# A linear-attention block on one core: reordered head loads, q tiles and normaliser spread over the state stage, a permuted Wo round trip, and a split last tile

## The chip, the cores and the metric

The kernel runs on one core of a Trainium2 chip. The metric is device time in microseconds (us). A profiled run also gives the span, from the first to the last instruction, which is 1.8 to 2.1 us shorter than the measured time; places in time below are us from the start of the span. TensorE does the matrix products, ScalarE the exponentials and part of the copies out of the accumulators, VectorE the rest; the sync engine (SP) and ScalarE issue transfers.

Each run of a changed kernel has runs of the kernel before beside it on the same chip. A run more than 1.5% above the fastest of its kernel is set aside as slow. Some kernels below do or do not fall to half TensorE clock in mid-kernel from run to run; for those I give the median of all runs as well, because the label then separates two behaviours of the kernel itself.

## The reference

```python
# x: (1, 2048, 640) bf16; wqkv: (640, 1920); wo: (640, 640); 32 heads of 20
qkv = (x @ wqkv) -> q, k, v per head
phi = lambda t: where(t > 0, t + 1, exp(t)) + 1e-6
kv  = einsum("bhsd,bhse->bhde", phi(k), v)
z   = sum over s of phi(k)
o   = einsum("bhqd,bhde->bhqe", phi(q), kv) / (einsum("bhqd,bhd->bhq", phi(q), z) + 1e-6)
out = o (heads joined) @ wo
```

## The kernel before

It never forms v. It sums P = x^T phi(k) over the rows (the state stage), gets kv = P^T Wv per group of six heads, masks it to 20x20 blocks, and folds it into Wo, so that the output is one product of the normalised phi(q) with the folded matrix. The stages on TensorE are: head (transposes of the first four row tiles, first key products), K stage (key products), state in two halves, kv and Wo groups with q tiles between them, output.

```python
def load_wk():                      # head loads on two queues
    for eng, what in (("act", "x0 w0 w2 w4 x2"), ("sp", "x1 w1 w3 x3")):
        ...                         # then the activation table

def p_step(h, st):                  # one state step: 5 products into banks 0 to 4
    for d in range(5): matmul(bank(d), xn[st, d], pk[st, half h])

def w2_rows():                      # folded Wo: to memory and back with rows regrouped
    dma(w2d[0:600] <- w2g[0:120, 5 groups]); dma(w2d[600:640] <- w2g[0:40, group 5])
    for c in range(5):
        dma(w2p[:, c] <- w2d.rearrange("(h c j) n -> c h j n", c=5, j=4)[c])

warm(5); transpose_x(0, 6); transpose_x(1, 7); warm(2)
for c in range(5):                  # first 20 key products, weight chunk by weight chunk
    for st in range(2):
        for h in range(2): k_half(st, h, (c,))
    if c >= 3: transpose_x(c - 1, c + 3)
```

The round trip through memory is there because the q side keeps its columns in the order (chunk c, head h, j) while the folded matrix comes out in the order (h, c, j).

Of the kernel before, what the change touches and what calls it, by code (L numbers as in the profile page):

```python
# [82 lines left out]
def bass_standalone__linear_attn_block__prompt_kernel(nc, x, wqkv, wo, out):  # L83
# [9 lines left out]
    BK = 512  # L93

    with contextlib.ExitStack() as ctx:
# [26 lines left out]
        bm = sb("bm", GW)  # L122
        ones = sb("ones", 8, F32)
# [23 lines left out]
        def pool_const():  # L147
# [10 lines left out]
            P.add("pool", lambda e: e.memset(bm[:, :], 1.0), writes=["bm"])  # L158
# [17 lines left out]
            for lo in (True, False):  # L176
                band(bm[:, :], [[-DH if lo else DH, NG], [0, DH]],
                     0 if lo else DH - 1, 1 if lo else -1, "bm")
# [8 lines left out]
        def load_xT():  # L187
            for i, (a, b) in enumerate(XCH[NPE:]):
                P.add("sp", lambda e, a=a, b=b: e.dma_start_transpose(
                    xT[:, :].rearrange("p (c s) -> p c s", s=S)[:, :, a:b], x[0, a:b, :]),  # L190
                    reads=[("wk", 0)] if i == 0 else [],
                    writes=[("xT", NPE + i)], dma=True)

        def transpose_x(st, b):
            v = bank(b, HALF).bitcast(BF16)

            def mm(e):
                for c in range(NC_):
                    r = e.transpose(v[:, 128 * c:128 * c + 128],  # L199
                                    xn[:, st * D + 128 * c:st * D + 128 * c + 128], ident[:, :])  # L200
                return r
            P.add("pe", mm, reads=[("xn", st), "ident"], writes=[("bank", b)])
            P.add("dve", lambda e: e.tensor_copy(  # L203
                xT[:, :].rearrange("p (c s) -> p c s", s=S)[:, :, 128 * st:128 * st + 128],
                v.rearrange("p (c s) -> p c s", s=128)),
                reads=[("bank", b)], writes=[("xT", st)])

        def xT_keys(a, b):
            return [("xT", i) for i, (p, q) in enumerate(XCH) if p < b and a < q]
# [13 lines left out]
        def load_wk():  # L223
            for eng, what in (("act", "x0 w0 w2 w4 x2"), ("sp", "x1 w1 w3 x3")):
# [8 lines left out]
            tl = mybir.InstLoadActFuncSet(  # L233
                name=nc.get_next_instruction_name(),
                act_func_set_id=ACT_TABLE_SET_LN_EXP, ins=[], outs=[])
            P.add("act", lambda e: e.add_instruction(tl), writes=["table"])
# [28 lines left out]
        def k_half(st, h, cs=range(NC_)):  # L265
# [10 lines left out]
            P.add("pe", mm, reads=xT_keys(128 * st, 128 * st + 128) + [("wk", c) for c in cs],  # L276
# [16 lines left out]
        def p_step(h, st):  # L293

            def mm(e):
                for d in range(NC_):
# [6 lines left out]
                  writes=[("bank", d) for d in range(NC_)])  # L303

        def p_out(h):
            for d in range(NC_):
                dst = pt[:, d * D + HALF * h:d * D + HALF * (h + 1)]
                if d % 2 == 0:
                    P.add("act", lambda e, d=d, dst=dst: e.copy(dst, bank(d, HALF)),  # L309
                          reads=[("bank", d)], writes=[("pt", d, h)])  # L310
                else:
                    P.add("dve", lambda e, d=d, dst=dst: e.tensor_copy(dst, bank(d, HALF)),
                          reads=[("bank", d)], writes=[("pt", d, h)])
# [70 lines left out]
        def kv_group(b):  # L384

            for lo, hi, bb in ((0, 4, b), (4, 6, b + 1)):
                def mm(e, lo=lo, hi=hi, bb=bb):
                    for g in range(lo, hi):
                        n = gsz[g]
                        m = 128 if g < 5 else n  # L390
                        for d in range(NC_):
# [3 lines left out]
                                pt[:, d * D + GW * g:d * D + GW * g + n],  # L395
# [5 lines left out]
            for lo, n, bb, w, key in ((0, 4, b, GW, 0), (4, 1, b + 1, GW, 1), (5, 1, b + 1, 40, 2)):  # L401
                src = ps[0:w, BK * bb + 128 * (lo % 4):BK * bb + 128 * (lo % 4) + 128 * n] \
                    .rearrange("p (g j) -> p g j", j=128)[:, :, 0:w]
                mk = bm[0:w, 0:w].unsqueeze(1).broadcast_to([w, n, w])
                dst = kvt[0:w, GW * lo:GW * (lo + n)].rearrange(
                    "p (g j) -> p g j", j=GW)[:, :, 0:w]
                P.add("dve", lambda e, src=src, mk=mk, dst=dst: e.tensor_tensor(
                    dst, src, mk, ALU.mult), reads=[("bank", bb), "bm"], writes=[("kvt", key)])

        def w2_group(g, b):  # L410
            n = gsz[g]
            for h in range(2):
# [3 lines left out]
                    reads=[("kvt", 0 if g < 4 else g - 3), "wog", "wog5"],  # L416
                    writes=[("bank", b + h)])
            P.add("act", lambda e: e.copy(
                fold(w2g[0:n, g * D:(g + 1) * D]), two_banks(b, parts=n)),
                reads=[("bank", b), ("bank", b + 1)], writes=[("w2g", g)])  # L420

        def w2_rows():
            P.add("sp", lambda e: e.dma_start(
                w2d[0:5 * GW, :].rearrange("(g p) n -> p g n", p=GW),
                w2g[0:GW, 0:5 * D].rearrange("p (g n) -> p g n", n=D)),
                reads=[("w2g", g) for g in range(5)], writes=["w2d"], dma=True)
            P.add("sp", lambda e: e.dma_start(
                w2d[5 * GW:D, :], w2g[0:gsz[5], 5 * D:6 * D]),
                reads=[("w2g", 5)], writes=["w2d5"], dma=True)
            for c in range(NC_):  # L430
                P.add("sp", lambda e, c=c: e.dma_start(
                    w2p[:, c * D:(c + 1) * D],
                    w2d.rearrange("(h c j) n -> c h j n", c=NC_, j=4)[c]),
                    reads=["w2d", "w2d5"], writes=[("w2p", c)], dma=True)
# [34 lines left out]
        def normalize(sbk):  # L469
            i = sbk % 2  # L470
            for c in range(NC_):
                v = pq[:, c * S + BK * sbk:c * S + BK * (sbk + 1)]
                P.add("dve", lambda e, v=v: e.tensor_tensor(v, v, rd[i][:, :], ALU.mult),  # L473
                      reads=[("rd", i), ("pq", sbk, c)], writes=[("pq", sbk, c)])

        def out_tile(st):
            b = 2 * (st % 4)
            j = st % 4
            for h in range(2):
                def mm(e, h=h):  # L480
                    for c in range(NC_):
                        r = e.matmul(bank(b + h, HALF),  # L482
                                     pq[:, c * S + 128 * st:c * S + 128 * st + 128],
                                     w2p[:, c * D + HALF * h:c * D + HALF * (h + 1)],
                                     start=(c == 0), stop=(c == NC_ - 1))
                    return r
                P.add("pe", mm, reads=[("pq", st // 4, c) for c in range(NC_)]
                      + [("w2p", c) for c in range(NC_)], writes=[("bank", b + h)])
            P.add("act", lambda e: e.copy(osb[j][:, 0:HALF], bank(b, HALF)),  # L489
                  reads=[("bank", b)], writes=[("osb", j, 0)])  # L490
            P.add("dve", lambda e: e.tensor_copy(osb[j][:, HALF:D], bank(b + 1, HALF)),  # L491
                  reads=[("bank", b + 1)], writes=[("osb", j, 1)])
            P.add("sp", lambda e: e.dma_start(
                out[0, 128 * st:128 * st + 128, :], osb[j][:, :]),
                reads=[("osb", j, 0), ("osb", j, 1)], writes=[("out", st)], dma=True)
# [7 lines left out]
        warm(5)  # L503
        transpose_x(0, 6)
        transpose_x(1, 7)
        warm(2)
        for c in range(NC_):
            for st in range(2):
                for h in range(2):
                    k_half(st, h, (c,))  # L510
            if c >= 3:
                transpose_x(c - 1, c + 3)
# [8 lines left out]
        qi = [0]  # L521

        def next_q(b):
            q_tile(*qs[qi[0]], b)
            qi[0] += 1

        for h in range(2):
            for st in range(NT):
                p_step(h, st)
                if zst and st % 2 == 1:  # L530
                    zst.pop(0)()
                if st == 7:
                    next_q(5 + qi[0] % 3)
            p_out(h)
            next_q(5 + qi[0] % 3)
            next_q(5 + qi[0] % 3)
        for f in zst:
            f()
        kv_group(0)
        next_q(5)  # L540
        z_finish(4)
        w2_group(0, 2)
        next_q(6)
        w2_group(1, 0)
        den(0, 4)
        den_act(0, 4)
        next_q(7)
        w2_group(2, 2)
        den_spread(0, 4)
        next_q(5)  # L550
        w2_group(3, 0)
        normalize(0)
        next_q(6)
        w2_group(4, 2)
        next_q(7)
        w2_group(5, 0)
        den(1, 4)
        w2_rows()
        den_act(1, 4)
        next_q(5)  # L560
        next_q(6)
        den_spread(1, 4)
        normalize(1)
        while qi[0] < 15:
            next_q((7, 2, 3, 5, 6)[qi[0] % 5])
        next_q(0)
        next_q(1)
        den(2, 4)
        den_act(2, 4)
        next_q(2)  # L570
        next_q(3)
        den_spread(2, 4)
        normalize(2)
        next_q(5)
        for st in range(2):
            out_tile(st)
        den(3, 6)
        den_act(3, 6)
        out_tile(2)
        den_spread(3, 6)  # L580
        normalize(3)
        for st in range(3, NT):
            out_tile(st)
# [4 lines left out]
        def _(e):  # L588
            P.emit("sp", e)
            for s in range(NT):  # L590
                op = P.writers[("out", s)]
# [45 lines left out]
```

## Time and profile before

| | before |
|---|---|
| time, median of 4 runs | 109.47 us |
| span of the profiled run | 107.7 us |
| TensorE busy, mean clock | 92%, 1.0 |
| first product of key tile 2 / first state product / first kv product | 9.19 / 29.03 / 57.56 |
| last q product done / first output product / last output product done | 81.00 / 81.00 / 104.86 |

The last two rows are milestones that I take from the timeline of TensorE. They are how the two kernels are compared below, because the work between two milestones can be counted. Their lines (start, length, group; the one at 9.19 is cut off by the end of its window):

```profile
5.88 2.38 PE L270 MATMUL ps<-wk,xT 128*128 128x320 bf16 x16
...
9.19 7.09 PE L270 MATMUL ps<-wk,xT 128*128 128x320 bf16 x51
...
29.03 5.61 PE L297 MATMUL ps<-pk,xn 128*128 128x320 bf16 x40 [0.66 <-DVE pk L288]
...
57.56 1.70 PE L392 MATMUL ps<-pt,wv 128*128 128x120 bf16 x30
...
79.92 1.24 PE L323 MATMUL ps<-xT,wqp 128*128 128x512 bf16 x5
81.00 2.88 PE L482 MATMUL ps<-w2p,pq 128*128 128x320 bf16 x20
```

### The profile page before, as it was taken

How to read it: one execution, taken by the hardware profiler on the slowest of the kernel's cores; microseconds unless marked ns; L12 is line 12 of the kernel's file. 1: busy time of each engine (PE TensorE's matmuls, PEld its weight loads, DVE VectorE, ACT ScalarE, POOL GpSimd, SP SyncE). 2: the span in 40 equal slices, each digit the busy share in tenths (PEclk: the TensorE clock that was granted, in tenths of full speed). 3: DMA queues.
4: the chain of work that ended last, by engine and by line, in shares of the span. 5: the costliest groups of instructions: out<-in, count | busy, mean ns of one | idle time of the engine just before them, and what ended most of it. 6: DMA issues, size and time to landing. Idle time of an engine off the chain costs nothing.

```text
span 107.7 us, 1890 instructions
## 1 busy us (share of the span) xinstructions
PE 99.6 (92%) x749; PEld 64.8 (60%) x755; DVE 68.2 (63%) x136; ACT 41.3 (38%) x77; POOL 10.7 (10%) x27
## 2 busy tenths in 40 slices
PE   5899999999799999999999999985999879999990
PEld 2467777777476674676767745432446557777760
DVE  1216998888899899701236674999879583333331
ACT  0404555555500206202035289872665433333330
POOL 6881000191000000000000000000000000000000
PEclk9999999999999999999999999999999999999999
DMA  2998999999980000000000000082730222333333
GB/s 52 370 203 190 223 145 213 383 366 363 266 161 0 0 3 0 0 0 6 0 0 3 0 0 6 14 215 75 194 111 0 85 104 85 119 117 125 118 120 115
DMA packets 16330, 12.24 MB, mean 114 GB/s; under 512 B 8386, under 2 KB 16322, under 8 KB 16322
## 3 DMA queue, kind: packets, MB, share of 16 engines
q1 hardware_dynamic: 15602, 11.31, 38.6%
q10 hardware_dynamic: 720, 0.82, 2.2%
q8 instruction: 6, 0.10, 0.4%
q14 instruction: 2, 0.02, 0.1%
HBM read 6.72 MB, written 3.44 MB: 94 GB/s over the span
## 4 chain that ended last, share of the span: by engine, by line
PE 75%; DVE 13%; ACT 5%; DMA 3%; issue 1%
PE ps L270 19%; PE ps L482 18%; PE ps L297 15%; PE ps L323 15%; DVE za L342 4%; DVE pq L336 3%; DMA xn<-in_x_dram 3%; ACT eq L331 3%; PE ps L199 2%; DVE pq L473 2%; PE ps L441 2%; PE ps L392 1%; DVE eq L333 1%; ACT rd L466 1%; PE ps L373 1%
## 5 line engine op out<-in xcount | busy, mean ns | idle before, releaser
L323 PE MATMUL ps<-xT,wqp 128*128 128x512 bf16 x94 | 22.9, 379 | 1.8 <-DVE pq L336 1.5
L297 PE MATMUL ps<-pk,xn 128*128 128x320 bf16 x160 | 22.4, 299 | 0.8 <-DVE pk L288 0.7
L482 PE MATMUL ps<-w2p,pq 128*128 128x320 bf16 x160 | 22.2, 299 | 0.7 <-ACT rd L466 0.7
L270 PE MATMUL ps<-wk,xT 128*128 128x320 bf16 x160 | 22.3, 299 | 0.0
L297 PEld LDWEIGHTS ps<-pk,xn 128*128 128x128 bf16 x160 | 15.5, 98 | 7.9 <-DVE pk L288 1.0
L331 ACT ACTIVATE eq<-ps 128x512 bf16<-128x512 f32 x20 | 11.9, 597 | 21.4 <-PE ps L323 21.3
L482 PEld LDWEIGHTS ps<-w2p,pq 128*128 128x128 bf16 x160 | 15.5, 98 | 7.0 <-ACT rd L466 0.8
L270 PEld LDWEIGHTS ps<-wk,xT 128*128 128x128 bf16 x160 | 15.7, 98 | 6.4 <-issue 0.6
L283 ACT ACTIVATE ek<-ps 128x640 bf16<-128x640 f32 x16 | 11.2, 704 | 13.5 <-PE ps L270 13.5
L323 PEld LDWEIGHTS ps<-xT,wqp 128*128 128x128 bf16 x100 | 9.3, 98 | 11.0 <-DVE pq L336 1.9
L491 DVE CAST osb<-ps 128x320 bf16<-128x320 f32 x16 | 7.8, 490 | 11.5 <-PE ps L482 11.5
L336 DVE SCALAR_TENSOR_TENSOR pq<-ps,eq 128x512 bf16<-128x512 f32 x20 | 13.8, 692 | 0.7
L288 DVE SCALAR_TENSOR_TENSOR pk<-ps,ek 128x640 bf16<-128x640 f32 x16 | 13.2, 825 | 0.5
L333 DVE TENSOR_SCALAR eq<-eq 128x512 bf16<-128x512 bf16 x20 | 5.8, 292 | 10.9 <-ACT eq L331 10.4
L489 ACT CAST osb<-ps 128x320 bf16<-128x320 f32 x16 | 6.8, 426 | 13.2 <-PE ps L482 13.1
L473 DVE TENSOR_TENSOR pq<-pq,rd 128x512 bf16<-128x512 bf16 x20 | 7.0, 418 | 0.3 <-ACT rd L466 0.3
L285 DVE TENSOR_SCALAR ek<-ek 128x640 bf16<-128x640 bf16 x16 | 5.4, 335 | 1.7 <-ACT ek L283 1.6
L203 DVE COPY xT<-ps 128x640 bf16<-128x640 bf16 x4 | 2.0, 492 | 6.7 <-PE ps L199 6.6
L309 ACT CAST pt<-ps 128x320 bf16<-128x320 f32 x6 | 2.2, 434 | 9.7 <-PE ps L297 9.7
L342 DVE TENSOR_TENSOR za<-pk 128x1280 f32<-128x1280 bf16 x4 | 5.7, 1484 | 0.0
L253 POOL COPY wqp<-wqn 128x640 bf16<-128x640 bf16 x5 | 3.7, 773 | 12.6 <-DMA wqn<-in_wqkv_dram 12.6
L261 PE MATMUL ps<-zero 128*128 128x512 bf16 x7 | 3.4, 630 | 1.3 <-DVE eps L155 1.3
(40 smaller groups left out, 47.6 us busy)
## 6 DMA issues: line engine op xcount, KB each, us to landing
out_dram<-osb SPq DMA_DIRECT2D x16, 160.0 KB, 1.8
xn<-in_x_dram SPq DMA_DIRECT2D x3, 640.0 KB, 7.7
wqn<-in_wqkv_dram SPq DMA_DIRECT2D x1, 800.0 KB, 5.3
wv<-in_wqkv_dram SPq DMA_DIRECT2D x1, 800.0 KB, 10.7
w2p<-w_rows SPq DMA_DIRECT2D x5, 160.0 KB, 2.7
wog<-in_wo_dram SPq DMA_DIRECT2D x1, 750.0 KB, 13.0
w_rows<-w2g SPq DMA_DIRECT2D x1, 750.0 KB, 5.3
wk<-in_wqkv_dram ACTq DMA_DIRECT2D x3, 160.0 KB, 3.9
```

The source lines that it names most:

```text
L270: r = e.matmul(bank(b + h, HALF), xT[:, c * S + 128 * st:c * S + 128 * st + 128], wk[:, c * D + HALF * h:c * D + HALF * (h + 1)], start=(c ...
L283: P.add("act", lambda e: e.activation(fold(t[:, :]), two_banks(b), ACTF.Exp), reads=banks + ["table"], writes=[("ek", st % 3)])
L288: P.add("dve", lambda e: e.scalar_tensor_tensor(fold(pk[:, st * D:(st + 1) * D]), two_banks(b), 0.0, fold(t[:, :]), ALU.max, ALU.add), rea ...
L297: r = e.matmul(bank(d, HALF), xn[:, st * D + 128 * d:st * D + 128 * d + 128], pk[:, st * D + HALF * h:st * D + HALF * (h + 1)], start=(st ...
L323: r = e.matmul(bank(b), wqp[:, d * D + 128 * c:d * D + 128 * c + 128], xT[:, d * S + BK * sbk:d * S + BK * (sbk + 1)], start=(d == 0), sto ...
L331: P.add("act", lambda e: e.activation(t[:, :], bank(b), ACTF.Exp), reads=[("bank", b), "table"], writes=[("eq", i)])
L333: P.add("dve", lambda e: e.tensor_scalar(t[:, :], t[:, :], 1.0, 1e-6, ALU.min, ALU.add), reads=[("eq", i)], writes=[("eq", i)])
L336: P.add("dve", lambda e: e.scalar_tensor_tensor(pq[:, c * S + BK * sbk:c * S + BK * (sbk + 1)], bank(b), 0.0, t[:, :], ALU.max, ALU.add), ...
L342: P.add("dve", lambda e: e.tensor_tensor(d_ap, a, b, ALU.add), reads=ra + rb, writes=[dst])
L473: P.add("dve", lambda e, v=v: e.tensor_tensor(v, v, rd[i][:, :], ALU.mult), reads=[("rd", i), ("pq", sbk, c)], writes=[("pq", sbk, c)])
L482: r = e.matmul(bank(b + h, HALF), pq[:, c * S + 128 * st:c * S + 128 * st + 128], w2p[:, c * D + HALF * h:c * D + HALF * (h + 1)], start=( ...
L491: P.add("dve", lambda e: e.tensor_copy(osb[j][:, HALF:D], bank(b + 1, HALF)), reads=[("bank", b + 1)], writes=[("osb", j, 1)])
```

## The change

It has four aims. The head loads are to come in the order of need. Idle TensorE time around the state stage is to be filled with q tiles and the first normaliser. The folded Wo is to be read back as whole rows. And the end is to be shortened by splitting the last tile in three. The core of the diff, with cuts:

```diff
-            for eng, what in (("act", "x0 w0 w2 w4 x2"), ("sp", "x1 w1 w3 x3")):
+            P.add("act", lambda e: e.add_instruction(tl), writes=["table"])
+            for eng, what in (("sp", "x0 w0 x1 w1"), ("act", "w2 w3 w4 x2 x3")):
...
-                    reads=[("wk", 0)] if i == 0 else [],      # gate of the transposing transfers
+                    reads=[("wk", 2)] if i == 0 else [],
...
+        p_step(0, 0, range(4)); p_step(0, 1, range(4)); p_step(0, 0, (4,)); p_step(0, 1, (4,))
...        # 11 q tiles, the z sums, the denominator and spread of block 0 inside the state stage
...
+        def w2_write(g):                                      # one write per group
+            w2d.rearrange("(c r) n -> c r n", c=NC_)[:, 24 * g:24 * g + w, :] <- w2g[0:gsz[g], group g]
+        def w2_read(lo, hi):                                  # two reads, chunks 0-2 and 3-4
+            w2p[chunks lo..hi] <- w2d[128 * lo:128 * hi, :]   # waits for all six writes
...
-        warm(5)
+        warm(4)
         transpose_x(0, 6)
-        transpose_x(1, 7)
-        warm(2)
+        warm(1)
+        for st, cs in ((0, (0,)), (1, None), (0, (1, 2)), (1, (0, 1, 2)), (0, (3, 4)), (1, (3, 4))):
+            # None: the second transpose; else key products of tile st, chunks cs
+        transpose_x(2, 6)
+        transpose_x(3, 7)
```

To make whole rows possible, the copies of the state out of the accumulators (pt) now write the order (chunk, row), so a group's partitions also come in the order (chunk, row).

## The prediction

> **What bounds the kernel now.** I read the page first, then the list of waits by engine, the timeline in order of time, and last the landings of single transfers. The page's busy rows and the mean clock come first:
>
> ```profile
> PE 99.6 (92%) x749; PEld 64.8 (60%) x755; DVE 68.2 (63%) x136; ACT 41.3 (38%) x77; POOL 10.7 (10%) x27
> PE   5899999999799999999999999985999879999990
> DVE  1216998888899899701236674999879583333331
> PEclk9999999999999999999999999999999999999999
> ```
>
> TensorE is busy in nearly every slice and at the full granted clock, so the time is its work plus its holes, plus a head before its first useful product and a tail after its last. VectorE is full only in the K stage (slices 5 to 17) and again between about 66 and 84 us. So I count TensorE's work and then its holes. The timeline of TensorE alone (start, length, group) gives starts:
>
> ```profile
> 43.45 5.61 PE L297 MATMUL ps<-pk,xn 128*128 128x320 bf16 x40
> 48.89 1.24 PE L323 MATMUL ps<-xT,wqp 128*128 128x512 bf16 x5
> 49.97 5.60 PE L297 MATMUL ps<-pk,xn 128*128 128x320 bf16 x40
> ...
> 71.89 0.39 PE L462 MATMUL ps<-rdc,em 128*128 128x128 bf16 x4
> 73.80 3.41 PE L323 MATMUL ps<-xT,wqp 128*128 128x512 bf16 x14 [1.52 <-DVE pq L336]
> ...
> 84.20 0.46 PE L441 MATMUL ps<-pq,zb 128*32 128x128 bf16 x20 [0.32 <-DVE pq L336]
> ...
> 87.03 17.83 PE L482 MATMUL ps<-w2p,pq 128*128 128x320 bf16 x130 [0.68 <-ACT rd L466]
> ```
>
> From start to start: 40 state products (x against phi(k)) take 48.89-43.45 = 5.44, so one step of 5 takes 0.68; a q tile takes 49.97-48.89 = 1.08; an output tile (17.83-0.15)/13 = 1.36, the 0.15 being the last product's own latency; the K tiles also 1.36 (exponentials come every 1.36 us). In the same way the other groups give 1.63 for all kv products, 1.04 for the z sums, 0.27 for each of 6 Wo groups, 0.40 for each of 4 denominators, 0.23 for each of 4 spreads. Work from the first K product on: 16x1.36 + 32x0.68 + 20x1.08 + 1.63 + 1.04 + 1.62 + 1.60 + 0.92 + 16x1.36, and 0.56 for two of the four transposes, is 94.2 us. The first K product starts at 5.88 and the last output product ends at 104.86: 98.98 us. The holes are therefore near 4.7 us, and the list of waits names them:
>
> ```profile
> PE ps L323 <- DVE pq L336: 1.5, 1, 1.5
> PE ps L482 <- ACT rd L466: 0.7, 1, 0.7
> PE ps L297 <- DVE pk L288: 0.7, 1, 0.7
> ```
>
> By starts they are: 0.8 between the K stage and the first state step (28.2 to 29.03), 0.3 at the turn to the second half of the state (43.15 to 43.45), 0.35 in small pieces near 63 and 69, 1.7 before the q products at 73.80, 0.1 at 77, 0.5 before the last denominator at 84.20, and 0.8 at 87.03, where the output waits for the last normaliser. Sum 4.55. The head is 5.88 us and the tail 107.66-104.86 = 2.8 us.
>
> [...] the warm-up products here take 0.42 us apart against 0.216 later, so an earlier head runs partly cold. [...] here the 512-wide combine from PSUM takes 692 ns, and splitting it over time makes it no cheaper. [...] the small output writes land after 1.8 us and the read-backs after 2.7, which is what each leg of the Wo round trip must pay.
>
> **The change, part by part.** *Head.* In the trace the nine head loads land 0.45 us apart, from 3.76 (x1) and 3.94 (x0) to 7.4 (x2)[...]. After, the activation table (1.28 us) goes first on the second queue. If it holds that queue, x0 w0 x1 w1 have the transfers to themselves and w2 w3 w4 x2 x3 follow. I put x0 at 3.5 (estimate: its own 0.45 instead of a shared one). Before, the copy of x0's transpose began 0.8 after its landing; a copy of 2 of 5 blocks takes about 0.29 instead of 0.49 (from 492 ns for 640 elements, less a fixed 0.16 as in the other PSUM forms). First K product: 3.5+0.8+0.29+0.1 = 4.7 instead of 5.88. But the gain is spent at once. The second transpose now lies behind it, some products run cold, and tiles 2 and 3 are transposed after all 20 head products with nothing to cover their copies: 0.5 transposition to copy, then 0.65. I get K tile 2 at 9.15 to 9.6, against 9.19 before. Beyond it stands another gate, the transposing transfer of rows 512 to 1023:
>
> ```profile
> L189 SPq DMA_TRANSPOSE xT<-in_x_dram x1: 3909/3909/3909, 4.8 to 4.8; - x1
> DMA to landing us min/median/max: 6.8/6.8/6.8
> ```
>
> It lands at 11.6 and is needed at 11.9. Now it starts on w2's landing (about 5.3) instead of w0's (4.77), so it lands about 11.9. Head: 0, within half a us either way. I shade it to a gain of 0.2.
>
> *K to state.* The first two steps take banks 0 to 3 first (8 products, 1.09 us) and bank 4 afterwards, when pk of tile 14, which held it, is done (28.98). The 0.8 hole closes: -0.8.
>
> *State.* It takes 3+2+4+2 = 11 q tiles before kv instead of 6, and the z sums, denominator and spread of block 0. That moves 5x1.08+1.04+0.40+0.23 = 7.1 us of TensorE work earlier and saves none. VectorE keeps up: per q tile 0.29+0.69+gaps = 1.02, a za addition 1.42 to 1.48, between q tiles 2.7 to 4 us apart. Its last work before the half turn ends within 0.05 of what TensorE needs, so of the 0.3 there nothing to 0.3 is won: -0.25. The normaliser's reciprocal is no longer behind anything: -0.1.
>
> *kv and Wo.* From kv on 9 q tiles remain instead of 14. Six 120-row groups are evacuated alternately by ScalarE (0.69) and by both (0.43 and 0.44). In my ledger group 3 and group 5 each wait about 0.3 for VectorE: +0.5, against 0.25 of small holes before. kv starts about 63.6, the last Wo evacuation ends about 72.0. Its write lands about 73.9 (1.8, as the output rows); the two reads (800 KB at 0.43 per 160 KB is 2.15, plus 2.3) land about 78.4. TensorE has after group 5 six q tiles, two denominators and two spreads, 6x1.08+0.8+0.46 = 7.7 us, so it arrives at 78.2 to 78.4. A tie; I take +0.1. The pool engine's 20 short mask selections (0.4 to 0.6 each) end near 17, before its permutation at 21.08.
>
> *q stage.* The 1.7 hole goes: it was VectorE's backlog of five consecutive normalisations (1.76) plus tiles in front of a bank. After, two normalisations go between tiles, 1.02+0.70 = 1.72 a tile, against TensorE's 1.08. VectorE falls behind but four rotating banks absorb it, except about 0.2. The backlog comes out at the end: q tile 19 is done on VectorE near 81.9, while TensorE, after output tiles 0 and 1 (78.5+2.72), wants the last denominator at 81.2: a hole of 0.7, where 0.5 was. -1.7+0.2+0.2 = -1.3.
>
> *Last normaliser.* Tiles 2 and 3 now stand between denominator and spread, and block 1 follows: -0.8.
>
> *Tail.* The last copy is 160 columns (about 0.3) instead of 0.49, with its own transfer: -0.2.
>
> Sum, in the order above: -0.2 (head) -0.8 -0.25 -0.1 (state) +0.25 (groups) +0.1 (round trip) -1.3 -0.8 -0.2 = -3.3. From the median of 109.51 that is 106.2.
>
> **The rivals.** (1) *The head is lost.* If the table does not hold the second queue, w2 w3 w4 land before x1 and w1, which then come near 5.4 and 6.4 instead of 4.4 and 4.8; tile 2 starts 0.75 late: 107.0. If it holds it for longer than 1.28, w2 lands after 6 and the transposing transfer after 13: TensorE waits over 1 us at tile 4, 107.4. For it: that transfer has only 0.3 us of slack. Against: the order looks made for a hold of just that length. (2) *The Wo round trip becomes the bound.* Before, 12 us lay between its first write (68.91) and the first output (81.00), and the q tiles covered them; now 6.5 do. If small writes take 3.2 us like the first output rows, the output waits 1.4 more, of which 0.7 replace the wait on VectorE: 106.9. (3) *VectorE is the bound of the q stage.* Its 10 us of backlogged work then shift output by a further 1 us: 107.2. (4) *All holes close and the head gains its 1.2*: 109.5-4.55-1.2-0.2 = 103.6. Against it speaks the 0.3 of slack.
>
> **Range and chances.** Terms certain from the trace (K to state, q hole, last normaliser) are 2.9; new holes and the head spread by about 0.8 each, independent. Predicted 106.2, range 104.4 to 107.9. Two per cent is 2.2 us, at 107.3: 0.8 faster, 0.18 the same, 0.02 slower.
>
> **What would show it.** Right: the wait of the state products on pk gone; no wait of the first product of output tile 4 on rd; the longest TensorE wait in mid-kernel at the last denominator or at the first output, under 1 us; K tile 2 within 0.5 us of 9.2; the last output product ending 3.1 us earlier. Wrong: K tile 4 waiting on a transfer, or an output product waiting over 1 us on the read-back.

## The result

The changed kernel takes 112.94 us (112.23 to 113.74, 4 runs), the kernel before 109.47. The ratio is 1.032, 95% interval 1.023 to 1.042: slower. A ratio is the mean of one kernel's fast runs over the mean of the other's of the same rounds, so not quite the ratio of the medians. I had predicted 106.2 with 104.4 to 107.9. The profiled run is the slowest of the four (113.74), so the terms read from its trace are likely on the high side of what the change costs.

Busy share and granted clock of the changed kernel, in 40 slices as on the page before:

```profile
PE   5789899999999999999999999999935999999991
PEclk9999999999999999999999999999998599999999
```

There is a hole in TensorE at slices 29 and 30, about 81 to 86 us, that was not there, and right after it the clock is not full. TensorE's waits name it (total, times, longest):

```profile
PE ps L505 <- DMA w2p<-w_rows: 3.2, 1, 3.2
...
PE ps L281 <- DVE xT L208: 0.4, 1, 0.4
```

The three waits shown before (on pk, on VectorE's pq in front of the q products, on the normaliser) are gone, as intended; one wait on the read-back stands in their place. That alone does not explain the time, so here is TensorE's timeline (start, length, group), where L281 is the key products, L203 the transposes, L308 the state, L337 q tiles, L505 the output:

```profile
6.86 4.55 PE L281 MATMUL ps<-wk,xT 128*128 128x320 bf16 x18 [0.15 <-DMA wk<-in_wqkv_dram]
11.25 0.72 PE L203 MATMUL ps<-ident,xn 128*128 128x128 bf16 x10
12.34 19.19 PE L281 MATMUL ps<-wk,xT 128*128 128x320 bf16 x140 [0.37 <-DVE xT L208]
31.37 3.56 PE L308 MATMUL ps<-pk,xn 128*128 128x320 bf16 x25
...
66.73 1.70 PE L406 MATMUL ps<-pt,wv 128*128 128x120 bf16 x30
...
80.75 1.24 PE L337 MATMUL ps<-xT,wqp 128*128 128x512 bf16 x5
85.19 4.55 PE L505 MATMUL ps<-w2p,pq 128*128 128x320 bf16 x20 [3.20 <-DMA w2p<-w_rows]
...
93.02 16.48 PE L505 MATMUL ps<-w2p,pq 128*128 128x320 bf16 x125
```

Two groups have wrong durations. Eighteen key products take 4.55 us in the head, 0.25 each, where the 140 that follow take 0.136 each. Twenty output products take 4.55 where 125 take 16.48 (0.136 each, the last ten half as long). In both places TensorE runs at half speed for most of the group: in the trace the single products start 0.267 us apart up to 10.84 us and 0.136 apart after it, and again 0.267 apart between 85.93 and 89.34. Below I call TensorE cold at the half pace and warm at the full one. The page's clock row shows only the second, because the trace's clock records begin with the full-clock stretch at 10.84 and a time without a record is printed as full. Against the milestones of before:

| stretch | before | after | difference |
|---|---|---|---|
| to key tile 2 | 9.19 | 12.34 | +3.15 |
| to the first state product | 19.84 | 19.03 | -0.81 |
| to the first kv product, less the 7.1 us moved in | 28.53 | 28.26 | -0.27 |
| to the last q product's end, with the 7.1 us moved out | 16.34 | 15.10 | -1.24 |
| to the first output product | 0.00 | 3.36 | +3.36 |
| to the last output product's end | 23.86 | 24.31 | +0.45 |
| tail | 2.80 | 2.40 | -0.40 |
| span | 107.7 | 111.9 | +4.2 |

Before, the stretch of 23.44 us from kv to the last q product held the 7.1 us that moved. The middle of the kernel gained 2.3 us; the head and the round trip lost 6.5; the output lost a little although its own holes had closed.

Why is the head late? ScalarE's own timeline shows the first step of the answer:

```profile
0.81 1.28 ACT L238 ACT_TABLE_LOAD   x1 [0.81 <-PEq L703]
0.85 1.36 ACTq L245 DMA_DIRECT2D wk<-in_wqkv_dram  x3
```

The table loads from 0.81 to 2.09, and the queue of the same engine issues w2, w3 and w4 from 0.85 on. The table holds nothing. So w2 (landed at 3.92) and w3 (5.17) are under way together with x0 (3.74) and w0 (4.71), and x1 lands at 5.95 and w1 at 6.81 (before: 3.76 and 4.51; single landings are the last completion mark of each transfer in the trace). The round trip shows in the chain of waits that ended last:

```profile
75.29 5.28 DMA w_rows<-w2g
...
81.15 3.90 DMA w2p<-w_rows
```

The last evacuation of w2g ends at 75.25, close to where the ledger had it (72.0 plus the head's 3.1). Then the writes need 5.3 us where I had allowed 1.9. They land one after the other at 74.47, 76.08, 77.65, 78.91, 80.15 and 80.56. The two reads take 4.4 us, as worked out.

### The profile page after: what moved, and what is told of

It is laid out like the page before. It is cut to its first block, busy times and chain, and to the rows that moved or that the text cites. A ratio compares the mean times of both kernels' runs of the same rounds, so it can differ in the third digit from the quotient of the medians.

```text
span 111.9 us, 1937 instructions
## 1 busy us (share of the span) xinstructions
PE 103.4 (92%) x758; PEld 65.8 (59%) x758; DVE 69.5 (62%) x143; ACT 40.9 (37%) x78; POOL 14.5 (13%) x46
## 4 chain that ended last, share of the span: by engine, by line
PE 80%; DMA 12%; DVE 2%; SPq 2%; ACT 1%; issue 1%
PE ps L281 21%; PE ps L505 21%; PE ps L308 20%; PE ps L337 14%; DMA w_rows<-w2g 5%; DMA wk<-in_wqkv_dram 4%; DMA w2p<-w_rows 3%; PE ps L406 1%; PE ps L387 1%; PE ps L432 1%; ACT eq L345 1%; SPq L229 1%; PE ps L468 1%; DVE pq L350 1%; DVE xT L208 1%
## 5 line engine op out<-in xcount | busy, mean ns | idle before, releaser
L505 PE MATMUL ps<-w2p,pq 128*128 128x320 bf16 (+1 forms) x165 | 23.9, 309 | 3.2 <-DMA w2p<-w_rows 3.2
L281 PE MATMUL ps<-wk,xT 128*128 128x320 bf16 x160 | 24.4, 317 | 0.6 <-DVE xT L208 0.4
L337 PE MATMUL ps<-xT,wqp 128*128 128x512 bf16 x100 | 24.4, 380 | 0.0
L308 PE MATMUL ps<-pk,xn 128*128 128x320 bf16 x160 | 23.7, 299 | 0.0
L505 PEld LDWEIGHTS ps<-w2p,pq 128*128 128x128 bf16 x165 | 16.4, 102 | 10.5 <-DVE pq L499 3.7
L281 PEld LDWEIGHTS ps<-wk,xT 128*128 128x128 bf16 x160 | 16.2, 103 | 8.6 <-DMA wk<-in_wqkv_dram 1.0
L308 PEld LDWEIGHTS ps<-pk,xn 128*128 128x128 bf16 x160 | 15.5, 98 | 7.2 <-DVE pt L326 0.2
L530 DVE CAST osb<-ps 128x320 bf16<-128x320 f32 (+1 forms) x16 | 7.7, 481 | 14.2 <-PE ps L505 14.2
L337 PEld LDWEIGHTS ps<-xT,wqp 128*128 128x128 bf16 x100 | 9.4, 98 | 9.2 <-issue 0.3
L527 ACT CAST osb<-ps 128x320 bf16<-128x320 f32 (+1 forms) x17 | 7.0, 417 | 17.0 <-PE ps L505 16.9
L208 DVE COPY xT<-ps 128x256 bf16<-128x256 bf16 (+1 forms) x8 | 2.1, 319 | 9.4 <-PE ps L203 9.4
L164 POOL TENSOR_SCALAR_AFFINE_SELECT bm<-bm 128x24 bf16<-128x24 bf16 (+1 forms) x20 | 4.3, 215 | 1.4
L356 DVE TENSOR_TENSOR za<-za 128x1280 f32<-128x1280 f32 x3 | 4.4, 1482 | 0.0
```

The costliest lines, as they stand in the source:

```text
L281: r = e.matmul(bank(b + h, HALF), xT[:, c * S + 128 * st:c * S + 128 * st + 128], wk[:, c * D + HALF * h:c * D + HALF * (h + 1)], start=(c ...
L308: r = e.matmul(bank(d, HALF), xn[:, st * D + 128 * d:st * D + 128 * d + 128], pk[:, st * D + HALF * h:st * D + HALF * (h + 1)], start=(st ...
L337: r = e.matmul(bank(b), wqp[:, d * D + 128 * c:d * D + 128 * c + 128], xT[:, d * S + BK * sbk:d * S + BK * (sbk + 1)], start=(d == 0), sto ...
L356: P.add("dve", lambda e: e.tensor_tensor(d_ap, a, b, ALU.add), reads=ra + rb, writes=[dst])
L505: r = e.matmul(bank(b, hi - lo), pq[:, c * S + 128 * st:c * S + 128 * st + 128], w2p[:, c * D + lo:c * D + hi], start=(c == 0), stop=(c == ...
L527: P.add("act", lambda e: e.copy(osb[j][:, lo:hi], bank(b, hi - lo)), reads=[("bank", b)], writes=keys)
```

## The experiments

The theory after reading the result has four parts: (a) the head costs 3.15 us, through late arrivals and through half clock; (b) the writes land late because of the shape of their target, which leads with the five chunks: the first 3.6 us after its issue, each further one of its size 1.2 to 1.6 us after the one before; (c) the idle 3.2 us drop the clock to half, which costs a further 1.7 us in the output; (d) the rest of the prediction holds. The rivals stand with each run. All runs gave correct results.

### The old head in the changed kernel (c1_oldhead)

```diff
-  sp: x0 w0 x1 w1 | act: table, w2 w3 w4 x2 x3 ; gate w2 ; two copies per tile ; new product order
+  the whole head of the kernel before
```

> The changed kernel with the whole head of the kernel before (loads of both queues in the old order, the activation table after the loads, the transposing transfer gated on w0, one copy per transposed tile, five and two warm-up products, the old order of the first key products). Theory: the head costs 3.15 us, because tile 2 of the key products starts at 12.34 instead of 9.19; everything after hangs on TensorE, so tile 2 returns to 9.2 and the time falls by 3.1, to about 109.8. Rival: the Wo round trip or VectorE sets the time of the output on its own, and a faster head is given back as a longer wait before the output: time within 0.5 of 112.9, the wait on the read-back growing from 3.2 to about 6.

Measured: median 110.18 of 12 runs, ratio 0.998 on the fast ones (0.993 to 1.003), against 1.032 for the unaltered change. TensorE's timeline:

```profile
8.89 19.18 PE L274 MATMUL ps<-wk,xT 128*128 128x320 bf16 x140
...
81.61 5.49 PE L498 MATMUL ps<-w2p,pq 128*128 128x320 bf16 x20 [3.08 <-DVE pq L492]
```

Key tile 2 is back, and a wait of about the same length as before stands in front of the output (the view names VectorE, which had come last by a little; the reads landed at 81.47). The head's loss is its own and was not hidden elsewhere. The rival, a wait grown to 6, falls. The 12 runs fall in groups by their mean clock: three at 1.0 took 108.58 to 109.19, eight at 0.984 took 110.03 to 110.68, and one at 0.969 took 111.26. The groups at 1.0 and at 0.984 lie some 1.5 us apart. The traced run, the one at 0.969, begins its output at half clock: 5.49 us for the 20 products that take 2.88 in the kernel before.

### The writes with 24 leading rows (c2_rmajor)

```diff
-  pt columns (chunk, row);  w2d "(c r) n -> c r n"[:, 24g:24g+24]   # target 5 x 24 x 640
+  pt columns (row, chunk);  w2d "(c r) n -> r c n"[24g:24g+24]      # target 24 x 5 x 640
```

> The changed kernel with the folded Wo written out of partitions in the order (row, chunk) instead of (chunk, row), so that the leading dimension of each write's target is 24 rows and not 5 chunks; bytes, number of writes, and the two whole-row reads stay the same; the block mask becomes the old single one. Theory: [...] the six writes land 1.2 to 1.6 us apart, the last at 80.56; now each lands about 2 us after its issue, the last near 77.5, the reads near 81.8, so the first output product waits under 0.5 instead of 3.2; and [...] the array does not fall to half clock in the first output tiles (1.75 us). Time down by 4 to 5, to about 108.3. Rival: writes to memory and their receipts are slow whatever the pattern: landing times and the 3.2 us wait stay, time 112.9.

Measured: 111.47, ratio 1.014 (1.008 to 1.019); down from 1.032, but not to 108.3. The wait on the read-back is gone and the clock stays at 1.0. Each write now has 13 completion marks in the trace where the five-chunk writes have 6; they land 0.8 to 1.0 us apart instead of 1.2 to 1.6 (0.3 and 0.4 for the small last one), and the last lands 2.2 us after its issue. So part (b) holds, and the rival falls. The rest of the gain was lost to something I had not expected. The copies of pt, in the view of that tile (min/median/max in ns):

```profile
L320 ACT CAST pt<-ps x6: 1133/1314/1356, 45.8 to 67.9; 128x320 bf16<-128x320 f32 x6
L323 DVE CAST pt<-ps x4: 1137/1190/1247, 46.7 to 67.1; 128x320 bf16<-128x320 f32 x4
```

In the changed kernel the medians are 432 and 484. Writing bf16 elements 10 bytes apart costs 2.5 to 3 times as much as writing runs of four, and TensorE waits 1.1 us for these copies at the half turn and 1.1 us again before kv.

### Dummy products in the wait before the output (c3_warmout)

```diff
+  14 x matmul(bank(0), zero, zero)      # before out_tile(0, 0)
```

> The changed kernel with 14 dummy products of 512 columns (0.2155 us each, 3.0 us) on TensorE between the last q tile and the first output tile, into a free bank: they fill the wait on the read-back and end before it. Theory: the first 20 output products took 4.55 instead of 2.9 us because the clock fell to half after the idle 3.2 us; with the wait filled, they take about 2.9 and the time falls by 1.6 to 111.3; mean clock 1.0 after the head. Rival: they are slow for another reason (transfers still under way, banks not free): no change, 112.9. Where a run of the changed kernel did not fall to half clock (one of the four so far had a mean of 1.0), it gains nothing there, so the mean gain may be nearer 1.2.

Measured: 111.40, ratio 1.012 (1.004 to 1.019), near the 111.3 expected. The output starts with

```profile
84.45 2.88 PE L505 MATMUL ps<-w2p,pq 128*128 128x320 bf16 x20
```

that is 2.88 us for the same 20 products instead of 4.55. All four runs have a mean clock of 1.0, but the trace of this run holds no clock record at all, so its 1.0 proves nothing; the pace of the products does. Part (c) is shown. For comparison the changed kernel in stretches of time (TensorE, weight loads, VectorE, ScalarE, GpSimd, then granted clock, transfer share, GB/s):

```profile
85.15:89.70 4.55, 4.51 (x24) 2.61 (x28) 1.16 (x3) 0.85 (x2) 0.00 (x0) 0.62 0.11 40
89.70:105.00 15.30, 15.30 (x134) 11.09 (x134) 7.74 (x18) 5.75 (x14) 0.00 (x0) 1.00 0.30 108
```

TensorE is "busy" for all of the first stretch, and only the clock column tells why it does so few products in it.

### More warm-up products in the head (c4_warmhead)

```diff
-  warm(4); transpose 0; warm(1); first products; transpose 1
+  warm(5); transpose 0; warm(1); first products; warm(1); transpose 1; warm(1)
```

> The changed kernel with three more warm-up products in the head's idle times (five instead of four before the first transpose, one on either side of the second transpose), loads as they are. Theory: the first 18 key products took 4.55 us, 0.25 each instead of 0.136, because the array was still at half clock after an idle head; with the gaps filled it is warm by about 6.5, they take about 2.5 to 3, and tile 2 starts 1.5 to 2 us earlier, time down 1.5 to 2 to about 111.2. Rival: the loads alone set the head (x1 lands at 5.95 and w1 at 6.81), or the added products only delay the queue: tile 2 stays at 12.3 or later and the time at 112.9.

Measured: median 112.63; two runs near 111.5 and two near 113.7, ratio of the faster two 1.015 (1.008 to 1.022). In the profiled run, one of the faster:

```profile
6.96 2.62 PE L281 MATMUL ps<-wk,xT 128*128 128x320 bf16 x18 [0.56 <-DMA wk<-in_wqkv_dram]
```

The 18 products take 2.62 instead of 4.55 and key tile 2 starts at 10.51 instead of 12.34, though w1 lands no earlier (6.91). So 1.8 us of the head's loss in the traced run are half clock, and the loads alone do not set it. That the filling made the array warm is not shown: two of the four runs are as slow as the slowest of the change, and e2_groupread_newhead below, which has the change's own head without the filling, is warm in its trace too.

### Old order of rows, a write per group (d1_natural)

```diff
-  pt columns (chunk, row); target 5 x 24 x 640; two reads of whole rows
+  old head; pt in the old order; w2d[120g:120g+120, :] <- w2g group g; the five old reads
```

> The changed kernel with the old head (as in the run that restored it) and with the Wo round trip in the old order of rows: head-major rows everywhere, one write per group into 120 contiguous rows, then the five old reads in runs of four rows. Theory: a write with 120 leading rows [...] lands about 2 us after its issue, at one evacuation of w2g after the other; the last near 73.8 against 77.1, the five reads take 5.3 as in the kernel before, last near 79.1; the last q tile ends on TensorE at 78.4, so the wait falls from 3.1 to about 0.7, there is no fall to half clock, and the evacuations of pt stay at 0.43 and 0.48 us. Time 2.5 to 3.5 below the run with the old head: about 106.3, ratio to before 0.97. Rival: writes this small are slow whatever their target: 109.5.

Measured: 106.72 (106.64 to 106.86), ratio 0.974 (0.969 to 0.978). Each write of 120 contiguous rows has 16 completion marks and lands 2.0 us after its issue; the wait before the output is 0.6. Expected 106.3 and a wait of 0.7. The size of the writes was not the trouble.

### A read per group behind its write (d2_groupread)

```diff
-  w2d "(c r) n -> c r n"[:, 24g:24g+24] <- w2g          # five leading chunks
-  two reads that wait for all six writes
+  old head; w2d[120g:120g+120, :] <- w2g                # contiguous, in the order (chunk, row)
+  w2p[24g:24g+24] "r (c n)" <- w2d[120g:120g+120] "(c r) n -> r c n"   # waits for write g alone
```

> The changed kernel with the old head, the changed order of rows inside a group kept (so the cheap copies in runs of four columns stay), each group written to 120 contiguous rows, and one read per group which gathers its five chunks into 24 partitions (8 for the last) as soon as that group's write has landed, instead of two reads that wait for all six writes. Theory: only the last small read stands behind the last write: 73.8 + about 2 = 76 to 77, before the last q tile ends at 78.4; no wait for the read-back at all, and the output then waits for VectorE (last denominator, under 1 us). Time about 106.0, ratio 0.965, a few tenths below the run with five reads. Rival: reads into 24 partitions are slow[...], or the queue is blocked by the early reads' waits and delays the later writes: the wait stays over 2 us, time above 108.

Measured: 106.29 (106.10 to 106.85), ratio 0.970 (0.965 to 0.975), the best of the study and 3% below the kernel before. TensorE goes from the last q tile into the output without a wait:

```profile
78.92 0.38 PE L330 MATMUL ps<-xT,wqp 128*128 128x512 bf16 x1
79.22 2.88 PE L497 MATMUL ps<-w2p,pq 128*128 128x320 bf16 x20
82.05 0.46 PE L460 MATMUL ps<-pq,zb 128*32 128x128 bf16 x20
```

The last read lands at 78.87, later than the 76 to 77 expected, because the reads into 24 partitions land up to 1.7 us apart; it is still in time. With one head and one round trip put right, this is the time that I had predicted for the change. To the tenth it is luck: tile 2 starts at 9.66 here, where I had counted on a gain of 0.2 from 9.19, and the hole before the last denominator is 0.1 instead of 0.7.

### The old loads alone (d3_oldloads)

```diff
-  sp: x0 w0 x1 w1 | act: table, w2 w3 w4 x2 x3 ; gate w2
+  act: x0 w0 w2 w4 x2, table | sp: x1 w1 w3 x3 ; gate w0
```

> The changed kernel with the loads alone as before (queues, order, table last, the transposing transfer gated on w0); split copies, warm-up products and the new order of the head's products stay. Theory: the arrivals are what spoiled the head: x1 lands near 3.8 instead of 5.95 and w1 near 4.5 instead of 6.8, so the 20 head products run from about 5 without long idle times; tile 2 starts at 9.2 to 9.8 and the time falls by 2.5 to 3, to about 110. Rival: the order of the products (second transpose behind the first product, tiles 2 and 3 transposed with nothing beside them) is the cause: tile 2 stays above 11, time above 112.

Measured: 112.18, ratio 1.024 (1.019 to 1.029). Key tile 2 starts at 11.12: earlier than 12.34, far from the 9.2 to 9.8 that I expected. x1 landed at 3.73 and w1 at 4.48, so the arrivals were mended, and the theory that they alone spoil the head falls. Of the 1.22 that tile 2 gains, 0.47 is the earlier start of the 18 products (6.39 instead of 6.86); the other 0.75 comes from the pace, which becomes full at 8.81 instead of 10.84. The numbers are those that I had written for the rival, the order of products. But the 18 products still took 3.81 us, that is mostly half clock, so the rival was not shown either; the next run on the head separates them.

### All head loads on one queue (d4_onequeue)

```diff
-  sp: x0 w0 x1 w1 | act: w2 w3 w4 x2 x3
+  sp: x0 w0 x1 w1 w2 w3 w4 x2 x3
```

> The changed kernel with the nine head loads on one queue in the order that was wanted: x0 w0 x1 w1 w2 w3 w4 x2 x3, the other queue empty. It tests whether a true order gives what the prediction counted on. Theory: they land 0.45 us apart from 3.5 to 7.2, x1 near 4.5 and w1 near 5; tile 2 starts at 9.2 to 9.8, time about 110. Rival: one queue cannot issue or carry as fast as two, the last loads land after 8, and the transposing transfer starts later and holds tile 4: time above 111.

Measured: median 110.80 of 20 runs, ratio of the fast ones 0.996 (0.993 to 0.999); nearly all runs with a mean clock of 0.984 or 0.985 are among the slow ones, in the traced run because of half clock in the output (4.55 us for its first 20 products). The order that the change wanted, made true:

```profile
9.46 2.89 PE L281 MATMUL ps<-wk,xT 128*128 128x320 bf16 x20 [0.26 <-DVE xT L208]
12.61 1.67 PE L281 MATMUL ps<-wk,xT 128*128 128x320 bf16 x11 [0.26 <-DMA xT<-in_x_dram]
```

Key tile 2 at 9.46 is inside the 9.15 to 9.6 of the prediction. But this head is warm from 4.07 us on. Against the trace of e2_groupread_newhead below, which is warm as well and starts tile 2 at 10.61, the true order is worth 1.15. One queue is also slower here than two, as the rival said: the loads land 0.7 apart, from 3.06 to 8.70, where on two queues before they landed 0.45 apart. Tile 4 then waits for the transposing transfer, which now starts on w2 at 6.14 and lands at 12.57. Both theories have a share: the order helps, and that gate takes back 0.3 to 0.4 of it. Even a true order is no faster than the old head.

### Old loads and filled head (e1_loads_fill)

```diff
+  old loads; warm(5) instead of warm(4), warm(2) instead of warm(1)
```

> The changed kernel with the old loads (as in the run with the old loads alone) and also two more warm-up products, one before and one after the first transpose, to fill TensorE's idle time in the head. The two causes of the head's loss so far, seen by the start of tile 2: new loads unfilled 12.34, new loads filled 10.51, old loads unfilled 11.12; the old head stands at 9.2. Theory: late arrivals and half clock are separate causes, and the new order of products adds a third, small one (tiles 2 and 3 transposed with nothing beside them, 0.4 to 0.9). So tile 2 at 9.8 to 10.2, the 18 products after the second transpose near 2.6 us instead of 3.8, time near 111.2. Rival: the order of products costs nothing, and tile 2 comes at 9.2 to 9.4; or the array stays at half clock in spite of the filling, and tile 2 stays above 11.

Measured: median 110.75 of 20 runs, ratio of the fast ones 0.9973 (0.9951 to 0.9995). In the profiled run, which is a slow one because of the output's clock (5.49 us for its first 20 products), the array is warm from 7.39 us on (16 products in 2.40 us) and key tile 2 starts at 10.58. That is later than the 9.8 to 10.2 expected: w2 landed at 7.21 in this run and held the queue for 0.4 us. From the first product of the last two transposes to tile 2 it takes 1.10 us, as in every run with the new order (1.09 in the changed kernel); the old order spends 0.56 there, because key products cover one copy. So the order of products is a third cause, of about 0.5.

### The repaired round trip with the new head (e2_groupread_newhead)

```diff
   as d2_groupread, but with the changed kernel's own head
```

> The changed kernel with nothing but the Wo round trip altered as in the best run so far (each group written to 120 contiguous rows, one read per group behind its write); its own new head stays. Theory: head and round trip are independent terms: this is the best run (106.3) plus the head's loss of 3 us, 109.3, ratio to before 0.995 to 1.005, with no wait for the read-back and a full clock in the output. Rival: the round trip's repair also shortens something in the head or hides part of its loss: time under 108; or the loss returns elsewhere, as another wait before the output: time above 111.

Measured: four runs at 107.27, 108.45, 109.14 and 109.97, all at a mean clock of 1.0; ratio of the two faster 0.984 (0.979 to 0.990), mean of all four 108.7. The profiled run is the fastest. Its head, which is the change's own, was warm:

```profile
7.06 2.62 PE L281 MATMUL ps<-wk,xT 128*128 128x320 bf16 x18 [0.67 <-DMA wk<-in_wqkv_dram]
...
10.61 4.66 PE L281 MATMUL ps<-wk,xT 128*128 128x320 bf16 x33 [0.37 <-DVE xT L208]
```

Tile 2 starts at 10.61, 0.95 later than in d2_groupread's profile; the run's time is 1.0 above that kernel's median. So the two terms add in this run, and the head's share is smaller when the array happens to be warm. In the three other traces with this head (the change, c2_rmajor, c3_warmout) it was cold, with tile 2 at 12.34, 12.48 and 11.95. I expected 109.3, which is where the slower runs lie. That those had a cold head is likely but not shown, as they have no trace.

### The split first state steps in the kernel before (e3_before_split)

```diff
-  p_step(0, 0); p_step(0, 1)
+  p_step(0, 0, range(4)); p_step(0, 1, range(4)); p_step(0, 0, (4,)); p_step(0, 1, (4,))
```

> The kernel before with one part of the change alone: the first two state steps take banks 0 to 3 first and bank 4 afterwards. Theory: the hole of 0.7 to 0.8 us between the K stage and the state closes and nothing takes it back, as TensorE is the bound of what follows until 72 us: time down by 0.6 to 0.8, ratio 0.993 to 0.995, the wait of the state products on pk gone. Rival: the 0.3 hole at the half turn (VectorE's za additions) grows by as much, because VectorE's work does not move: ratio 0.997 to 1.0.

Measured: 109.03 of 22 runs, ratio 0.9953 (0.9935 to 0.9971), or 0.5 us. TensorE's timeline at the half turn:

```profile
39.80 2.32 PE L323 MATMUL ps<-xT,wqp 128*128 128x512 bf16 x10
42.56 3.71 PE L297 MATMUL ps<-pk,xn 128*128 128x320 bf16 x26 [0.43 <-DVE pt L312]
```

The state's wait on pk is gone. But by starts the hole at the turn is now 42.56-(39.80+2x1.08) = 0.60, where it was 0.3: the state starts 1.17 us earlier (27.86 for 29.03, 0.35 of it from this run's head), but VectorE's additions end only 0.89 earlier (40.84 for 41.73). So of 0.8 won, 0.3 is given back in the old schedule, and both theories had a part. In the changed kernel, where those additions are spread out, nothing is given back.

## Why the prediction was wrong

It was wrong in direction. Two of its steps failed, and one consequence was left out; the others held.

**Head.** The step that failed is "If it holds that queue, x0 w0 x1 w1 have the transfers to themselves". The table held nothing: the second queue issued from 0.85. Rival (1) named this but priced it at 0.75, and the trace shows 3.15. The sum in the changed kernel's profile is: half clock 4.39-18x0.136 = 1.94 (6.86 to 11.25, against the warm rate); the transposes with nothing beside them 1.09-0.56 = 0.53; the remaining 0.68 is late arrival. The clock share is shown by the pace of the products and by the same head warm in e2_groupread_newhead (tile 2 at 10.61, 1.73 earlier), the order of products by e1_loads_fill, the arrival in part by d3_oldloads (0.47). I had noted the half pace of the warm-up products (0.42 us apart against 0.216 later) and then carried it as "some products run cold". It was the largest part of the head in this trace. Where the loads really came in order and the array was warm (d4_onequeue), tile 2 stood where the prediction put it.

**Round trip.** The failed step is "Its write lands about 73.9 (1.8, as the output rows)". An output row tile has 128 leading rows. The writes of the change lead with 5 in memory and 120 in the buffer. The completion marks differ with these shapes: 6 marks for 5 and 120, 13 for 24 and 120, 9 for the last group's 8 and 40, 11 for 40 and 40, 16 for 120 and 120 or for 128. In the change's first write one mark comes at 72.13 and the other five at 74.22 to 74.47, 3.6 us after its issue, and the six writes land 1.2 to 1.6 us apart (0.4 for the small last one); with 16 marks, in d1_natural, each landed after 2.0. From 72.5 to 80.0 us, with these writes under way, the 16 transfer engines were busy at a mean share of 0.32 and moved 107 GB/s; the two reads, from 81.2 to 85.0, came to 0.65 and 216. My estimate from the 0.32 is that about five engines' worth (0.32x16 = 5.1) carried the writes, and the same ones for all six, as the share stayed at 0.26 to 0.34 in each 2 us from 72 to 80 with several writes under way; which engines they were, no trace here shows. I had looked at the size of these writes and not at their shape. Rival (2) named this wait, but from slow single writes and not from six that land one after the other, and at 1.4 us, against 3.36.

**Left out: the clock after the wait.** The prediction speaks of a cold array in the head only; I gave no thought to the clock after a wait, here of 3.2 us. All six traces with a listed wait of 2.8 to 3.2 us before the output show half clock in it (4.50 to 5.49 us for the first 20 products instead of 2.88), and no wait of 1.5 or less is followed by it. It cost 4.55-2.88 = 1.67 us in this run, and by its mean clock nothing in the run at 1.0. The 0.7 us that the last denominator was to wait for VectorE does not appear: in d2_groupread VectorE is done with q tile 19 at 82.00, as the prediction had it (81.9), but TensorE arrives at 81.94 and not at 81.2.

**What held.** K to state: -0.8 predicted, -0.81 in the milestones (alone in the kernel before, 0.5). State: -0.35 predicted, -0.27 found. From kv to the last q product: +0.25 for the groups and -1.5 of the q stage's terms (its -1.3 less the last denominator's +0.2), together -1.25, found -1.24. Last normaliser: the output stretch of +0.45 is -1.22 once the half clock's 1.67 is taken out, against -0.8 for that term and -0.5 for the denominator's hole. Tail: -0.2 predicted, -0.4 found. VectorE did not become the bound (rival 3). One reading of the page was wrong: VectorE's row stays at 7 tenths or more to 45 us, so it is full through the first half of the state stage as well as in the K stage, which ends at 28.2; the term for the half turn had it right. d2_groupread, with the two failed parts put right, came to 106.29 against the predicted 106.2.

What stays open is how often the head starts cold, and whether more warm-up products help. Runs of c4_warmhead and of e2_groupread_newhead spread by 2.2 to 2.7 us. The moment of the change of clock differs from run to run: with the change's own head the clock records begin with full clock at 10.84 us in one run, 10.96 in another (c2_rmajor) and 4.74 in a third (e2_groupread_newhead), and half clock in the output lasts 3.41 us or twice that.

## What to carry to other kernels

Look at the leading sizes of a transfer on both sides before pricing it by its bytes: the writes of 150 KB with 120 and 120 landed 2.0 us after their issue here, while of those with 5 and 120 the first took 3.6 us and each further one 1.2 to 1.6 us more. A wait like those here (2.8 us and more) can be charged twice, once as the wait (3.2 us in the change) and once as half speed after it (1.67 us); compare the spacing of products, not busy time, in the head and after every long hole. And an order of loads over two queues is only an order if something really holds the second queue; the table load of 1.28 us did not, as w2 was issued 0.04 us after its start.
